# Reordering the first batch and cutting the last output tile in two halves instead of three pieces: linear attention followed by a gated feed-forward, one core

## The chip, the cores and the metric

The kernel runs on one core of a Trainium2 chip. The metric is device time in microseconds. Before the change the median of three runs is 296.06 us (295.66 to 296.08). Where the text gives a moment, it is in us from the start of the profiled span.

## What is computed

Eight batches of eight heads, 576 positions, 64 features a head. Cosine and sine weights of the position turn relu(q) and relu(k) into features of twice the width; attention is linear, so only a small matrix kv per head is needed. The result, one row of 512 per token, goes through a feed-forward with a gate.

```python
def phi(x, c, s):
    r = np.maximum(x, 0.0)
    return np.concatenate([r * c, r * s], axis=-1)
q_p = phi(q, cos_w, sin_w)
k_p = phi(k, cos_w, sin_w)
kv = np.einsum('bhsf,bhsd->bhfd', k_p, v)
z = np.sum(k_p, axis=2)
num = np.einsum('bhsf,bhfd->bhsd', q_p, kv)
den = np.einsum('bhsf,bhf->bhs', q_p, z)[..., None] + 1e-06
attn = num / den                       # then (tokens 4608, 512) as x
h = x @ w_in                           # 512 x 2048
g = h * (1.0 / (1.0 + np.exp(-beta * h)))
out = g @ w_out                        # 2048 x 512
```

## The kernel before

**Tiles and stages.** The 4608 tokens go through the feed-forward in nine chunks of 512. A chunk takes 32 slots: slots 0 to 15 make h for one of the 16 blocks of 128 columns of w_in (`h_mm`, four matmuls of 128x512 each, then a Silu on ScalarE, `h_act`), slots 16 to 31 multiply with w_out (`o_part`, four matmuls each; four parts for each of four token tiles, with the copy of the result by ScalarE and two stores after the fourth). Attention of the next batch is laid between those slots. In chunk 0 the parts come first: slots 16 to 19 use w_out slice 0 for all four tiles, 20 to 23 slice 1, 24 to 27 slice 2, 28 to 31 slice 3.

**Order.** The program's order is written out by hand; each engine works through its own instructions in that order and waits on semaphores. All loads and the last chunks' stores go through SP's queue, the other stores through GpSimd's.

**The first batch.** Nothing can be laid beside it, so its attention is written out in lines 420 to 491. The heads come in pairs: a pair jp has the heads 2jp and 2jp+1 of one half of the partitions, and the other half of the partitions (g) holds the other heads. A position is (partition, n) with n from 0 to 8. The pieces, for pairs 0 and 1:

- `v_scale` writes cos times v and sin times v (tile vb); `k_relu` writes relu(k) (tile rk); both are split over VectorE, ScalarE and GpSimd.
- `kv_mm` (line 254) multiplies them into kv: for every n two heads jj and two halves g, four matmuls of 64x64 with 130 columns, on the four quarters of the array. `kv_take` copies the result out of PSUM.
- `num_mm` multiplies the turned q with kv, `x_rden` (VectorE) forms the reciprocal of the denominator, `x_mul` (VectorE) or `x_mul_act` (ScalarE) the quotient xs, and `x_turn_pe` turns it on TensorE, with copies by ScalarE to xt, the input of h_mm.
- `warm_pe` issues matmuls of zeros in between whose result nobody reads.

**The weights of w_in.** Four slices of 512 columns (win0 to win3) come as f32 into a stage of four buffers (w_stage) and are cast to bf16 by `cast_win`. A slice is cast in pieces: gj = (g, jj) are the four pieces that hold all partitions, f0 to f1 the columns, jps the pairs of row blocks. The first two matmuls of an h_mm (mi = 0, 2) read the pieces with g = 0, mi = 1 and 3 those with g = 1. Slice 0 is cast by GpSimd, except for its last quarter; slices 1 to 3 by VectorE in halves of the columns (`cast_halves`, line 493): the first half of a slice serves two blocks jt, the second half the next two. The four slices of w_out use the same stage, slice i after w_in slice i has been cast out of its buffer; line 93 loads them, and `cast_wout` scales them to bf16.

**The last tile.** `o_last` (line 400) takes the last token tile of the last chunk in pieces of 256, 128 and 128 columns, each with 16 matmuls, a copy and two stores of 64 rows. Its stores go out on SP and on ScalarE's queue (`two=True`).

Of the kernel before, what the change touches and what calls it, by code (L numbers as in the profile page):

```python
# [17 lines left out]
NQ = 9  # L18
# [4 lines left out]
def kernel(  # L23
# [14 lines left out]
    nc = tc.nc  # L38
# [26 lines left out]
    ps = psum.tile([P, 8, 512], FP32, name="ps")  # L65
# [4 lines left out]
    def raw_tile(b, name):  # L70
        if (name, b) not in raws:
            raws[name, b] = raw_pool.tile([P, 4, NQ, D], FP32, name=f"raw_{name}", tag=f"raw_{name}")
        return raws[name, b]
# [24 lines left out]
    def cast_win(i, gj, eng="dve", f0=0, f1=512, jps=slice(0, 2)):  # L98

        g, jj = gj  # L100
        o = win[i].rearrange("q (jp g) f -> q jp g f", g=2)[jj * HP : (jj + 1) * HP, jps, g, f0:f1]
        a = stages["in", i].rearrange("q (jp jj) f -> q jp jj f", jj=2)[g * HP : (g + 1) * HP, jps, jj, f0:f1]
        if eng == "act":
            nc.scalar.copy(o, a)
        elif eng == "pool":
            nc.gpsimd.tensor_copy(o, a)
        else:
            nc.vector.tensor_copy(o, a)  # L108
# [11 lines left out]
    GJ = [(0, 0), (0, 1), (1, 0), (1, 1)]  # L120
# [65 lines left out]
    def relu(dst, src, eng):  # L186
        if eng == "act":
            nc.scalar.activation(dst, src, AF.Relu)  # L188
        else:
            nc.vector.tensor_scalar(dst, src, scalar1=0.0, scalar2=None, op0=ALU.max)  # L190

    def q_relu(b, jp, eng="dve"):
        relu(qb[:, jp].rearrange("q n (j d) -> q j n d", j=2), raw_tile(b, "q")[:, 2 * jp : 2 * jp + 2], eng)

    def k_relu(b, j0=0, j1=4, eng="dve", n0=0, n1=NQ):
        relu(rk.rearrange("q n j d -> q j n d")[:, j0:j1, n0:n1], raw_tile(b, "k")[:, j0:j1, n0:n1], eng)

    def v_scale(b, cs, jp=None, n0=0, n1=NQ, eng="dve"):
        t = (cos9, sin9)[cs]
        rv = raw_tile(b, "v")  # L200
        js = slice(0, 4) if jp is None else slice(2 * jp, 2 * jp + 2)
        if jp is not None and eng != "act":
            if eng == "dve":
                t = ps[:, 0, 16 * cs : 16 * cs + NQ]
            (nc.gpsimd if eng == "pool" else nc.vector).tensor_tensor(
                vb[:, n0:n1, js, cs, 0:D],
                rv.rearrange("q j n d -> q n j d")[:, n0:n1, js],
                t[:, n0:n1].unsqueeze(2).unsqueeze(3).to_broadcast([P, n1 - n0, 2, D]), op=ALU.mult)
            return
        for n in range(n0, n1):  # L210
            o, a = vb[:, n, js, cs, 0:D], rv[:, js, n, :]
            if eng == "act":
                nc.scalar.activation(o, a, AF.Copy, scale=t[:, n : n + 1])  # L213
            else:
                nc.vector.tensor_scalar(o, a, scalar1=t[:, n : n + 1], scalar2=None, op0=ALU.mult)  # L215
# [35 lines left out]
    def kv_out(jp, bank):  # L251
        return ps[:, bank : bank + 2, jp * 2 * E : (jp + 1) * 2 * E]

    def kv_mm(b, jp, bank, jjs=(0, 1)):
        t = kv_out(jp, bank)
        for n in range(NQ):
            for jj in jjs:
                for g in range(2):
                    hs = slice(g * HP, (g + 1) * HP)
                    nc.tensor.matmul(  # L260
                        t[jj * HP : (jj + 1) * HP, g], lhsT=rk[hs, n, 2 * jp + jj, :],
                        rhs=vb[hs, n, 2 * jp + jj].rearrange("q s e -> q (s e)"),
                        start=(n == 0), stop=(n == NQ - 1))

    def kv_take(jps, bank, eng="dve"):
        a0, a1 = jps[0], jps[-1] + 1
        o = kv[:, :, a0:a1].rearrange("q g s c e -> q g (s c e)")
        a = ps[:, bank : bank + 2, a0 * 2 * E : a1 * 2 * E]
        if eng == "act":
            nc.scalar.copy(o, a)  # L270
        else:
            nc.vector.tensor_copy(o, a)  # L272

    def num_mm(n, jp, bank, slot):

        for cs in range(2):
            for jj in range(2):
                rows = slice(jj * HP, (jj + 1) * HP)
                for g in range(2):
                    cols = slice(g * HP, (g + 1) * HP)  # L280
                    nc.tensor.matmul(  # L281
                        ps[cols, bank + jj, slot * E : (slot + 1) * E],
                        lhsT=(qt, qs)[cs][rows, jp, n, cols],
                        rhs=kv[rows, g, jp, cs, :],
                        start=(cs == 0), stop=(cs == 1))

    def x_rden(bank, slot, n0, n1, jps):

        w, m = len(jps), n1 - n0
        nv = ps[:, bank : bank + 2, slot * E : (slot + w * m) * E].rearrange("q j (i s e) -> q j i s e", s=w, e=E)  # L290
        den = small.tile([P, 2, m, w], FP32, name="den", tag=f"den{m}{w}")
        nc.vector.tensor_tensor(  # L292
            den, nv[:, :, :, :, D],
            eps9[:, n0:n1].unsqueeze(1).unsqueeze(3).to_broadcast([P, 2, m, w]), op=ALU.add)
        rden = small.tile([P, 2, m, w], FP32, name="rden", tag=f"rden{m}{w}")
        nc.vector.reciprocal(rden, den)
        return nv, rden, n0, jps
# [11 lines left out]
    def x_mul_act(got, n):  # L309
        nv, rden, first, jps = got  # L310
        for s_, jp in enumerate(jps):
            for jj in range(2):
                nc.scalar.activation(xs[:, n, jp, jj * D : (jj + 1) * D], nv[:, jj, n - first, s_, 0:D],
                                     AF.Copy, scale=rden[:, jj, n - first, s_ : s_ + 1])
# [64 lines left out]

    out_v = out.rearrange("(b p n) m -> b n p m", b=B, n=NQ)  # L380

    def store(c, tt, o_sb, m0=0, m1=512, two=False):
        for hf in range(2):
            bb, n = divmod((c * TCH + tt * P) // HP + hf, NQ)
            eng = (nc.sync, nc.scalar)[hf] if two else nc.sync if c >= 7 else nc.gpsimd
            eng.dma_start(out=out_v[bb, n][:, m0:m1], in_=o_sb[hf * HP : (hf + 1) * HP, m0:m1])  # L386

    def o_part(c, tt, part):
# [11 lines left out]
    def o_last(c, tt):  # L400

        o_sb = osb_pool.tile([P, DM], FP32, name="o_sb", tag="o_sb")
        for i, (m0, m1) in enumerate(((0, 256), (256, 384), (384, 512))):
            o_ps = ps[:, 4 + i, 0 : m1 - m0]
            for jt in range(JT):
                nc.tensor.matmul(o_ps, lhsT=gs[c, jt][:, tt * P : (tt + 1) * P],  # L406
                                 rhs=wout[jt // 4][:, jt % 4, m0:m1],
                                 start=(jt == 0), stop=(jt == JT - 1))
            (nc.scalar.copy if i == 1 else nc.vector.tensor_copy)(o_sb[:, m0:m1], o_ps)  # L409
            store(c, tt, o_sb, m0, m1, two=True)  # L410


    def warm_pe(count, w=512, bank=1):
        for i in range(count):
            nc.tensor.matmul(ps[:, bank, 0:w], lhsT=zeros[:, 0:P], rhs=zeros[:, 0:w], start=True, stop=True)  # L415
# [24 lines left out]
    warm_pe(7)  # L440
    take("act", 0)
    take("dve", 1)
    v_scale(0, 1, 0, 0, 6, eng="pool")
    take("act", 1)
    v_scale(0, 1, 0, 6, NQ, eng="act")
    v_scale(0, 0, 0)
    k_relu(0, 0, 2, "act", 0, 5)
    k_relu(0, 0, 2, "dve", 5, NQ)
# [4 lines left out]
    kv_take((0,), 6, eng="act")  # L453
    v_scale(0, 1, 1, 5, NQ, eng="act")
    k_relu(0, 2, 3, "act")
    k_relu(0, 3, 4, "act", 5, NQ)
    for i in range(1, 4):
        load_w("in", i)
    warm_pe(1)
    for n in range(7):  # L460
        num_mm(n, 0, 2, n)
    num_mm(7, 0, 4, 0)
    got = x_rden(2, 0, 0, 7, (0,))
    got2 = x_rden(4, 0, 7, 8, (0,))
    k_relu(0, 3, 4, "dve", 0, 5)
    warm_pe(2, bank=1)
    kv_mm(0, 1, 6)
    kv_take((1,), 6, eng="act")
    x_mul(got, 0, 7)
    x_mul_act(got2, 7)  # L470
    warm_pe(1, bank=1)
    for n in range(7):
        num_mm(n, 1, 0, n)
    num_mm(7, 1, 6, 0)
    for gj in GJ:
        cast_win(0, gj, "pool", jps=slice(0, 1))
    for gj in GJ:
        cast_win(0, gj, "pool", 0, 256, slice(1, 2))
    x_turn_pe(0, 0, 8, 2, jps=(0,))
# [1 line left out]
    x_mul(got, 0, 4)  # L481
    x_mul(got, 4, 7)
    x_mul(x_rden(6, 0, 7, 8, (1,)), 7, 8)
    warm_pe(3, bank=3)
    x_turn_pe(0, 0, 4, 4, ("act",), (1,))
    h_mm(0, 0, (0, 1))
    x_turn_pe(0, 4, 8, 5, ("act",), (1,))
# [5 lines left out]
    def cast_halves(i):  # L493
        for f in (0, 256):
            for gj in GJ:
                cast_win(i, gj, "dve", f, f + 256)
# [3 lines left out]
    def rest():  # L500

        x_mul(x_rden(2, 0, 8, NQ, (0, 1)), 8, NQ)
        cast_halves(2)
        cast_halves(3)
        load_w("out", 0)
        load_w("out", 1)
        load_raw(1, "v")
        load_raw(1, "k")
        load_w("out", 2)
        load_raw(1, "q")  # L510
        load_w("out", 3)
        cast_wout(0)
        cast_wout(1)
        v_scale(1, 0)
        k_relu(1)
        cast_wout(2)
        q_relu(1, 0)
# [111 lines left out]
```

## Time and profile before

| | us |
|---|---|
| median of three runs | 296.06 |
| profiled execution | 296.08 |
| its span | 294.27 |
| TensorE busy | 284.1 |
| idle of TensorE in the records from 18 us to the end, largest: before 56.58 | 0.49 |
| the same before 45.99 (w_out slice 3) | 0.22 |

| stretch, us | what runs | PE busy | DVE busy | ACT busy | POOL busy | DMA share |
|---|---|---|---|---|---|---|
| 7 to 12 | q turns, v and k of pair 0 | 3.69 | 4.46 | 3.65 | 1.47 | 1.03 |
| 12 to 17 | kv and num of both pairs | 3.98 | 3.83 | 3.28 | 3.22 | 1.04 |
| 17 to 33 | h of chunk 0 | 15.88 | 15.24 | 12.37 | 2.05 | 1.04 |
| 33 to 60 | output of chunk 0, batch 1 | 25.53 | 21.10 | 15.48 | 4.33 | 0.92 |
| 200 to 285 | last chunks | 84.52 | 9.08 | 40.05 | 12.64 | 0.28 |
| 285 to 295 | last tile, stores, end | 5.80 | 0.72 | 0.85 | 0.00 | 0.34 |

The loads of the first batch land one after the other: v of pair 0 at 8.80, k of pair 0 at 10.29, v of pair 1 at 12.07, k of head 2 at 12.73, of head 3 at 13.47, w_in slice 0 at 14.82 and 16.17, slices 1 to 3 at 18.87, 21.80 and 24.52; w_out slices at 27.36, 30.07, 38.78 and 45.19. A share of one in the table means that all 16 DMA engines work all the time. In the second table an engine's figure is its busy time within the stretch.

### The profile page before, as it was taken

To read this page: it belongs to the slowest core of one execution; us is meant where nothing else is said; L and a number is where in the kernel's file an instruction comes from. 1 tells how busy PE (TensorE), PEld (TensorE's weight loads), DVE (VectorE), ACT (ScalarE), POOL (GpSimd) and SP (SyncE) were. 2 spreads that over 40 slices of the span, in tenths; PEclk is the share of its full clock that TensorE was granted. 3 is DMA by queue.
4 is the path that set the end of the run, shared out by engine and by line. 5 is a ranking of instruction groups with operands and counts; after the bars stand their busy time and mean duration, and the time that the engine had idled before them with its cause. 6 is when DMAs were issued, how large, how long until landed. Compare 5 with 4: busy or idle time off the path is not lost.

```text
span 294.3 us, 7183 instructions
## 1 busy us (share of the span) xinstructions
PE 284.1 (97%) x3046; PEld 143.2 (49%) x3074; DVE 116.6 (40%) x297; ACT 140.1 (48%) x223; POOL 73.8 (25%) x88
## 2 busy tenths in 40 slices
PE   8799999999999999999999999999999999999995
PEld 7454455455444544454444544554455444444444
DVE  5989968662920294009500860077005000000000
ACT  5768826572248214831384128511761177127611
POOL 1350003252382026402460156014701210000000
PEclk9999999999999999999999999999999999999999
DMA  7999999597898089925992599239201910131033
GB/s 258 373 391 381 389 390 391 192 286 275 159 280 348 2 110 222 374 86 111 210 392 79 102 226 379 82 63 181 64 2 33 159 37 0 38 71 36 0 73 72
DMA packets 50416, 53.82 MB, mean 183 GB/s; under 512 B 30912, under 2 KB 31312, under 8 KB 50384
## 3 DMA queue, kind: packets, MB, share of 16 engines
q1 hardware_dynamic: 47424, 45.88, 51.7%
q0 software_dynamic: 2688, 7.34, 10.1%
q8 instruction: 24, 0.39, 0.5%
q10 hardware_dynamic: 272, 0.14, 0.2%
q14 instruction: 8, 0.07, 0.1%
HBM read 36.71 MB, written 9.44 MB: 157 GB/s over the span
## 4 chain that ended last, share of the span: by engine, by line
PE 84%; DVE 5%; DMA 5%; ACT 2%; issue 2%
PE ps L366 38%; PE ps L391 37%; DMA w_stage<-in_moe_w_out_dram 5%; DVE win L108 4%; PE ps L281 4%; PE ps L260 3%; PE ps L406 1%; PE ps L415 1%; ACT vb L213 1%; DVE qs L218 1%; DVE xs L303 0%; ACT g_t L373 0%; ACT rk L188 0%; PE ps L424 0%; PE ps L230 0%
## 5 line engine op out<-in xcount | busy, mean ns | idle before, releaser
L366 PE MATMUL ps<-xt,win 128*128 128x512 bf16 x576 | 128.1, 379 | 0.7 <-ACT g_t L373 0.5
L391 PE MATMUL ps<-wout,g_t 128*128 128x512 bf16 x535 | 120.4, 379 | 2.5 <-issue 1.4
L373 ACT ACTIVATE g_t<-ps,beta 128x512 bf16<-128x512 f32 x144 | 98.5, 688 | 36.5 <-PE ps L366 36.5
L366 PEld LDWEIGHTS <-win 128*128 128x128 bf16 x576 | 55.3, 98 | 67.5 <-DVE win L108 1.4
L391 PEld LDWEIGHTS <-g_t 128*128 128x128 bf16 x560 | 54.0, 98 | 64.0 <-issue 0.5
L386 POOL DMA_DIRECT2D out_dram<-o_sb x56 | 36.5, 656 | 142.2 <-ACT o_sb L397 142.2
L397 ACT COPY o_sb<-ps 128x512 f32<-128x512 f32 x35 | 20.5, 587 | 98.2 <-PE ps L391 98.2
L218 POOL TENSOR_TENSOR qs<-qt,tanr 128x1152 bf16<-128x1152 bf16 x12 | 29.2, 2456 | 10.3 <-DVE vb L215 8.9
L272 DVE CAST kv<-ps 128x520 bf16<-128x520 f32 x6 | 4.2, 699 | 67.8 <-PE ps L260 67.8
L409 DVE COPY o_sb<-ps 128x256 f32<-128x256 f32 (+1 forms) x2 | 0.7, 358 | 62.6 <-PE ps L406 62.6
L303 DVE TENSOR_TENSOR xs<-ps,rden 128x768 bf16<-128x768 f32 (+5 forms) x26 | 23.1, 890 | 0.8
L292 DVE TENSOR_TENSOR den<-ps,eps 128x12 f32<-128x12 f32 (+4 forms) x26 | 4.2, 161 | 33.5 <-PE ps L281 33.5
L215 DVE TENSOR_SCALAR vb<-raw_v,cos 128x256 bf16<-128x256 f32 x63 | 17.1, 348 | 0.0
L215 DVE TENSOR_SCALAR vb<-raw_v,sin 128x256 bf16<-128x256 f32 x54 | 14.7, 350 | 0.0
L281 PEld LDWEIGHTS <-qt 64*64 64x64 bf16 x576 | 10.6, 106 | 5.0 <-issue 4.3
L281 PE MATMUL ps<-kv,qt 64*64 64x65 bf16 x576 | 11.8, 194 | 0.4 <-ACT kv L270 0.2
L190 DVE TENSOR_SCALAR qb<-raw_q 128x1152 bf16<-128x1152 f32 x16 | 11.4, 753 | 1.3 <-DMA raw_q<-in_q_dram 1.3
L108 DVE CAST win<-w_stage 64x512 bf16<-64x512 f32 (+1 forms) x28 | 11.6, 413 | 0.6
L281 PE MATMUL ps<-kv,qs 64*64 64x65 bf16 x576 | 11.6, 193 | 0.0
L260 PE MATMUL ps<-vb,rk 64*64 64x130 bf16 x576 | 10.0, 218 | 1.6 <-ACT rk L188 1.6
L260 PEld LDWEIGHTS <-rk 64*64 64x64 bf16 x576 | 8.5, 106 | 5.6 <-issue 3.0
L281 PEld LDWEIGHTS <-qs 64*64 64x64 bf16 x576 | 10.4, 105 | 0.0
(56 smaller groups left out, 99.3 us busy)
## 6 DMA issues: line engine op xcount, KB each, us to landing
raw_v<-in_v_dram SPq DMA_DIRECT2D x7, 1152.0 KB, 10.3
raw_k<-in_k_dram SPq DMA_DIRECT2D x7, 1152.0 KB, 12.7
raw_q<-in_q_dram SPq DMA_DIRECT2D x7, 1152.0 KB, 7.5
out_dram<-o_sb POOLq DMA_DIRECT2D x56, 128.0 KB, 4.0
w_stage<-in_moe_w_out_dram SPq DMA_DIRECT2D x4, 1024.0 KB, 9.1
w_stage<-in_moe_w_in_dram SPq DMA_DIRECT2D x3, 1024.0 KB, 13.0
out_dram<-o_sb SPq DMA_DIRECT2D x14, 128.0 KB, 2.3
raw_q<-in_q_dram SPq DMA_DIRECT2D x2, 576.0 KB, 4.4
```

The source lines that it names most:

```text
L108: nc.vector.tensor_copy(o, a)
L190: nc.vector.tensor_scalar(dst, src, scalar1=0.0, scalar2=None, op0=ALU.max)
L215: nc.vector.tensor_scalar(o, a, scalar1=t[:, n : n + 1], scalar2=None, op0=ALU.mult)
L218: eng.tensor_tensor(dst.rearrange("q n (g p) -> q n g p", g=2), src.rearrange("q n (g p) -> q n g p", g=2), tanr[:, n0:n1].unsqueeze(2).to ...
L260: nc.tensor.matmul(t[jj * HP : (jj + 1) * HP, g], lhsT=rk[hs, n, 2 * jp + jj, :], rhs=vb[hs, n, 2 * jp + jj].rearrange("q s e -> q (s e)") ...
L281: nc.tensor.matmul(ps[cols, bank + jj, slot * E : (slot + 1) * E], lhsT=(qt, qs)[cs][rows, jp, n, cols], rhs=kv[rows, g, jp, cs, :], start ...
L303: nc.vector.tensor_tensor(o.rearrange("q j n s d -> q j (n s) d"), nv[:, :, a:z, :, 0:D].rearrange("q j n s d -> q j (n s) d"), rden[:, :, ...
L366: nc.tensor.matmul(ps[:, h_bank(c, jt)], lhsT=win[jt // 4][:, mi, (jt % 4) * P : (jt % 4 + 1) * P], rhs=xt[:, :, jp, g * HP : (g + 1) * HP ...
L373: nc.scalar.activation(g_t, ps[:, h_bank(c, jt)], AF.Silu, scale=beta[:, jt : jt + 1])
L386: eng.dma_start(out=out_v[bb, n][:, m0:m1], in_=o_sb[hf * HP : (hf + 1) * HP, m0:m1])
L391: nc.tensor.matmul(o_ps, lhsT=gs[c, jt][:, tt * P : (tt + 1) * P], rhs=wout[jt // 4][:, jt % 4, :], start=(jt == 0), stop=(jt == JT - 1))
L397: nc.scalar.copy(o_sb, o_ps)
```

## The change

Six edits. (1) `v_scale` of the sine of pair 0 is one GpSimd instruction over all n; before, GpSimd did n = 0 to 5 and ScalarE n = 6 to 8 in three. (2) `kv_mm` of pair 1 is called once for each head; the call for head 2 comes before the ScalarE part of `k_relu` for head 3 in the program, and before `x_rden`. (3) `x_mul_act` comes ahead of `kv_take` of pair 1. (4) One of the GpSimd casts of w_in slice 0 goes to ScalarE. (5) Two warm matmuls are left out. (6) The last slice of w_in is cast in four whole pieces instead of eight halves. The last output tile is computed in two pieces of 256 columns, the first copied by ScalarE and the second by VectorE, and all its stores go through SP.

```diff
-    def store(c, tt, o_sb, m0=0, m1=512, two=False):
+    def store(c, tt, o_sb, m0=0, m1=512):
         for hf in range(2):
             bb, n = divmod((c * TCH + tt * P) // HP + hf, NQ)
-            eng = (nc.sync, nc.scalar)[hf] if two else nc.sync if c >= 7 else nc.gpsimd
+            eng = nc.sync if c >= 7 else nc.gpsimd
             eng.dma_start(out=out_v[bb, n][:, m0:m1], in_=o_sb[hf * HP : (hf + 1) * HP, m0:m1])
...
-        for i, (m0, m1) in enumerate(((0, 256), (256, 384), (384, 512))):
-            o_ps = ps[:, 4 + i, 0 : m1 - m0]
+        for hf in range(2):
+            m0, m1 = 256 * hf, 256 * hf + 256
+            o_ps = ps[:, 4 + hf, 0:256]
             for jt in range(JT):
...
-            (nc.scalar.copy if i == 1 else nc.vector.tensor_copy)(o_sb[:, m0:m1], o_ps)
-            store(c, tt, o_sb, m0, m1, two=True)
+            (nc.scalar.copy if hf == 0 else nc.vector.tensor_copy)(o_sb[:, m0:m1], o_ps)
+            store(c, tt, o_sb, m0, m1)
...
-    v_scale(0, 1, 0, 0, 6, eng="pool")
+    v_scale(0, 1, 0, eng="pool")
     take("act", 1)
-    v_scale(0, 1, 0, 6, NQ, eng="act")
...
     k_relu(0, 2, 3, "act")
-    k_relu(0, 3, 4, "act", 5, NQ)
...
     num_mm(7, 0, 4, 0)
+    warm_pe(2, bank=1)
+    kv_mm(0, 1, 6, (0,))
+    k_relu(0, 3, 4, "act", 5, NQ)
     got = x_rden(2, 0, 0, 7, (0,))
     got2 = x_rden(4, 0, 7, 8, (0,))
     k_relu(0, 3, 4, "dve", 0, 5)
-    warm_pe(2, bank=1)
-    kv_mm(0, 1, 6)
+    kv_mm(0, 1, 6, (1,))
+    x_mul_act(got2, 7)
     kv_take((1,), 6, eng="act")
     x_mul(got, 0, 7)
-    x_mul_act(got2, 7)
-    warm_pe(1, bank=1)
...
     for gj in GJ:
-        cast_win(0, gj, "pool", jps=slice(0, 1))
+        cast_win(0, gj, "act" if gj == (1, 1) else "pool", jps=slice(0, 1))
...
-    warm_pe(3, bank=3)
+    warm_pe(2, bank=3)
...
         cast_halves(2)
-        cast_halves(3)
+        for gj in GJ:
+            cast_win(3, gj)
```

## The prediction

> **What bounds the kernel now.** I read the page first (busy shares, then the chain), then the first 50 us engine by engine in the timeline, the waits of the stretches that the change touches, and the last 8 us.
>
> ```profile
> PE 284.1 (97%) x3046; PEld 143.2 (49%) x3074; DVE 116.6 (40%) x297; ACT 140.1 (48%) x223; POOL 73.8 (25%) x88
> PE 84%; DVE 5%; DMA 5%; ACT 2%; issue 2%
> ```
>
> TensorE is busy 97% of the span and carries 84% of the chain. From about 18 us on it has hardly a gap, so the change can act in three places only: before 18 us, at the few waits of the first batch, and behind the last matmul. The waits of the first batch, by three views (waits of 25 to 34 us; chain of waits; timeline of PE):
>
> ```profile
> PEld L366 <- DVE win L108: 1.4, 4, 0.4
> ```
> ```profile
> 30.99 0.42 DVE win L108
> 31.41 0.03 issue
> 31.44 13.76 DMA w_stage<-in_moe_w_out_dram
> 45.20 0.02 issue
> 45.22 0.73 ACT wout L115
> ```
> ```profile
> 25.79 7.37 PE L366 MATMUL ps<-xt,win 128*128 128x512 bf16 x32
> 32.99 6.21 PE L391 MATMUL ps<-wout,g_t 128*128 128x512 bf16 x27
> ...
> 45.99 1.02 PE L391 MATMUL ps<-wout,g_t 128*128 128x512 bf16 x4 [0.22 <-ACT wout L115]
> ```
>
> Two things are to be seen. The weight loads of h_mm wait for VectorE's casts of w_in: in the single instructions jt 8 stands from 25.78 to 26.15, and each later pair of jt starts just as its half slice is ready (first half of slice 3 cast at 29.64, second matmul of jt 12 at 29.69). So VectorE and TensorE run neck and neck there. And at slot 28 PE stands 0.22 us for the last w_out slice. DMA is at 9 tenths in every slice from 26 to 50 us, moving 390 GB/s: that landing (45.2) is set by the bytes ahead of it.
>
> The casts that matter, timeline of DVE, then the two groups at 18.3 to 20 us:
>
> ```profile
> 18.50 5.07 DVE L108 CAST win<-w_stage 64x256 bf16<-64x256 f32 x12
> ...
> 24.36 7.05 DVE L108 CAST win<-w_stage 64x512 bf16<-64x512 f32 x16
> 31.45 1.67 DVE L117 TENSOR_SCALAR wout<-w_stage,rbeta 128x512 bf16<-128x512 f32 x4
> ```
> ```profile
> L108 DVE CAST win<-w_stage x4: 290/362/457, 18.5 to 19.7; 64x256 bf16<-64x256 f32 x4
> ```
> ```profile
> L106 POOL CAST win<-w_stage x3: 395/397/399, 18.0 to 18.9; 64x256 bf16<-64x256 f32 x3
> ```
>
> The four VectorE casts are alike, yet the first two take 457 and 431 ns and the others 290: the first two end 0.145 us behind a GpSimd cast each.
>
> **What the skill says.** SBUF — State Buffer, "SBUF: two separate sides": GpSimd and a VectorE operation in a 2-port mode exclude each other, whoever starts first keeps the pair for the whole instruction. The trace agrees with the casts just shown. VectorE: DVE Perf Modes, the perf-mode tier table: an fp32 copy inside SBUF runs at 2 elements a cycle; here 64x256 takes 290 ns and 64x512 421, which is 0.51 ns an element on 0.16 us fixed. TensorEngine Tiling, "Key Properties": tiles work independently; here the four 64x64 matmuls of one n start 3 ns apart and the next n 57 ns later. DMA: Bandwidth & Descriptors, "Issuing engines are not separate DMA queues": a second issuing engine saves only issue time; in the last pair of stores SP and ACT issue at 291.15 and 291.16, while SP alone starts its second store 0.51 us behind the first (288.47 after 287.96).
>
> **The change, part by part.**
>
> *sin of pair 0 all on GpSimd.* Its instruction grows from 768 to 1152 elements; the two shapes in the trace (1472 and 1257 ns) give 1.68 ns an element, so 2.12 us, 8.94 to 11.06 (2.2 at the mean rate). ScalarE loses three pieces (9.75 to 10.74), so its k_relu starts with the landing of k at 10.29 instead of 10.64 and ends at 11.04 instead of 11.37. But VectorE's own k_relu (512 elements, 10.41 to 10.83 now) falls under the longer GpSimd instruction; by the lock it ends about 0.27 behind it, at 11.33. kv_mm of pair 0 starts at 11.12, stands at n=5 until 11.39, and ends at about 11.8 instead of 12.12. Bounds: 0.33 early if it goes so, 0 if the whole k_relu comes after. I take 0.25.
>
> *kv of pair 1 by single heads.* Now: head 2 is ready on ScalarE at 14.30, the matmuls start at 14.35, head 3 joins at 14.49 behind VectorE's piece (14.43), the last one starts at 14.97. After: head 2 starts at 14.10. A head alone uses two of the four tiles, so nine n take 9 x 57 ns = 0.51 us as before, and the two heads come one after the other: 14.10 + 0.54 = 14.64, + 0.46 = 15.10, 0.13 later than now (0.05 at the best, 0.4 if the 0.25 is not there). x_mul_act, two instructions, moves ahead of kv_take and fits in the 0.62 us that ScalarE stands idle there. num_mm, x_rden and x_mul of pair 1 follow in a chain, so h_mm and VectorE's casts start 0.13 later.
>
> *One piece on ScalarE, 4th cast of slice 0.* 0.6 us behind kv_take (ends 15.7), done before the turn's copy at 17.0: free. GpSimd's remaining seven casts end at 18.59 instead of 19.26, and so VectorE's first two casts take 290 instead of 457 and 431: 0.31 us gained on VectorE; nothing if the GpSimd casts don't move up. Together the casts stand 0.17 earlier.
>
> *The warm matmuls* taken out (one before num_mm, one of three before the turn) lie in waits for ScalarE (kv, 15.61) and VectorE (xs, 17.53): nothing, as PEclk stays at 9 through the 1.1 us gap before 11.42.
>
> *Last slice in whole pieces.* Eight casts of 421 ns become four of 64x1024: 0.16 + 1024 x 0.51 = 0.68 us, with 0.02 between. They begin at 27.89 - 0.17 and all four are done after 2.81, at 30.53, 0.88 before now. But jt 12 needs the first half of all four pieces: its second matmul starts at 30.58 instead of 29.69. Behind it come 15 starts of 0.216 us: o_part begins at 33.82 instead of 32.99, PE 0.83 late. PE has no other gap until slot 28, where the wait of 0.22 goes first: 0.61 us remain. The w_out load of slice 3 is issued 0.9 earlier on SP, and the loads behind it too, but the engines are full, so it lands as now. All after slot 28 hangs on PE and moves with it.
>
> *The last tile.* 32 matmuls of 256 columns end at 290.76 (16 take 1.75) instead of 290.80. VectorE copies 256 columns, 425 instead of 292 ns, until 291.22; SP starts the first store at 291.25, the second at 291.76. A second store of 2 KB rows lands 2.37 us behind its start; rows of 1 KB land 0.29 faster (1.95 against 2.24 for first stores): 291.76 + 2.08 = 293.84, against 293.23 for ScalarE's last store now: + 0.61 (0.45 to 0.75). The stores of the first half go out before.
>
> Sum: 0.61 + 0.61 = 1.2 us on the profiled execution, 294.27 span and 1.81 around it, 296.08; that is the median of the runs too (296.06). Forecast 297.3.
>
> **Rivals.**
> *Full stall:* the k_relu of pair 0 comes wholly behind GpSimd, the heads serialise at + 0.38, and the casts gain only 0.15 from the lock: PE 1.2 late at o_part, 1.0 after the wait, plus 0.65: 297.7. For it: the lock. Against it: n=0 to 4 don't need the late piece.
> *Only the tail:* something on the way to slot 28 takes up the stall, or VectorE comes out 0.6 us further ahead: + 0.0 to 0.1 and 0.6, 296.7. Against it: no PE gap but 0.22 before slot 28.
> *Not slower:* the load of w_out slice 3 lands with its issue, as the chain draws it (13.76 us behind the cast), so 0.88 earlier, and single heads bring h_mm forward as well. Slot 28 could then start at 45.1. It decides only if PE is there, 0.67 before now, so h_mm must start at 17.3 instead of 18.0 and the jt 12 stall must vanish; less the tail this is 296.0. Against it: full DMA, and head 3's piece at 14.43, which lets the last kv matmul start 0.03 earlier at the most.
>
> **How the numbers follow.** Forecast 0.62, full stall 0.18, only the tail 0.14, not slower 0.06. The forecast's own ends are 296.8 and 297.7; 296.6 to 298.0 takes in most of the two slower rivals and leaves out about 1 in 10. About 0.2% (0.6 us) can be told from no change: "only the tail" lies on that line and gives half its chance to it, "not slower" a little: slower 0.86, same 0.09, faster 0.05.
>
> **What would show it.** A PE gap of about 1 us after the first matmul of jt 12, waiting for L108; the 0.22 wait for w_out gone and its landing still at 45.2; the first VectorE casts at 290 ns; the last kv matmul near 15.1; the two last stores 0.5 apart on SP. I am wrong if a 64x1024 cast takes well under 0.68, if the kv matmuls of a single head run closer than 57 ns per n, or if the landing moves with the issue.

## The result and the profile after

| | before | after |
|---|---|---|
| median of six runs, us | 295.69 | 297.09 |
| range of the runs | 295.62 to 296.08 | 296.80 to 297.21 |
| profiled execution | 296.08 | 297.13 |
| its span | 294.27 | 295.37 |

The ratio is 1.0042 (95% interval 1.0029 to 1.0055), so the change costs 1.24 us (0.86 to 1.63). Differences in us below are ratios worked out on the 295.7 to 296.1 us of the kernel before in the same series; those read from traces belong to one profiled execution each. One of all executions, the profiled one of everything but the tail (497.35 us at 0.56 of the clock), ran slow; it is left out, and its trace is not read.

The page of the kernel after, busy shares and the chain by engine:

```profile
PE 283.1 (96%) x3028; PEld 142.8 (48%) x3056; DVE 115.9 (39%) x292; ACT 140.0 (47%) x221; POOL 74.1 (25%) x87
...
PE 87%; DVE 4%; DMA 2%; issue 2%; ACT 2%; POOL 1%; SPq 0%; DVEq 0%; POOLq 0%
```

TensorE's busy time is all but the same, and it still carries most of the chain. DMA has lost 3 points of the chain: the step through the w_out landing, 13.76 us long, is gone. What stands there now, in the chain of waits from 29 to 46 us (start, length, what):

```profile
29.14 0.69 DVE win L108
29.84 0.70 DVE win L108
30.54 0.05 issue
30.59 3.41 PE ps L366 x15
```

The chain passes through the last two of the four whole pieces of w_in slice 3, 0.69 and 0.70 us each, and from there through TensorE alone. The timeline of PE over the same stretch (start, length, engine, line, operation, count; in brackets the idle time ahead and what ended it):

```profile
25.94 3.83 PE L366 MATMUL ps<-xt,win 128*128 128x512 bf16 x17
30.59 3.41 PE L366 MATMUL ps<-xt,win 128*128 128x512 bf16 x15 [0.82 <-DVE win L108]
33.84 6.21 PE L391 MATMUL ps<-wout,g_t 128*128 128x512 bf16 x27
...
45.59 1.94 PE L391 MATMUL ps<-wout,g_t 128*128 128x512 bf16 x8
```

Seventeen matmuls, the last of them the first one of jt 12, then 0.82 us of nothing, then the other fifteen. (The four matmuls of an `h_mm` run in the order mi = 0, 1, 2, 3, so the second is the first to read the pieces with g = 1; mi = 0 and 2 are not the first two, as the part on the kernel before has it.) Two things have changed against the kernel before: that gap is new, and the 0.22 that stood ahead of slot 28 is gone, for TensorE comes to slot 28 at 46.48 and the slice is ready. In starts of the same matmul, after is 0.84 late at the first `o_part` (33.835 against 32.991), 0.48 late at slot 28 (46.476 against 45.993), 0.51 late from 54 us and 0.40 late from 83 us on. The last tile adds 0.70, which makes the 1.10 by which the spans differ. How far single executions scatter is seen in the trace of the tail alone (below), whose first batch is that of before: it runs 0.34 ahead of the kernel before at 83 us.

The first 15 us. In the kernel before, the timelines of POOL and of DVE have

```profile
8.94 1.47 POOL L205 TENSOR_TENSOR vb<-raw_v,sin 128x768 bf16<-128x768 f32 x1 [6.78 <-DMA raw_v<-in_v_dram]
```
```profile
10.41 0.42 DVE L190 TENSOR_SCALAR rk<-raw_k 128x512 bf16<-128x512 f32 x1
```

and in the kernel after:

```profile
9.22 2.11 POOL L205 TENSOR_TENSOR vb<-raw_v,sin 128x1152 bf16<-128x1152 f32 x1 [7.06 <-DMA raw_v<-in_v_dram]
```
```profile
10.56 1.06 DVE L190 TENSOR_SCALAR rk<-raw_k 128x512 bf16<-128x512 f32 x1
...
12.27 1.34 DVE L205 TENSOR_TENSOR vb<-raw_v,ps 128x1152 bf16<-128x1152 f32 x1
...
14.11 0.47 DVE L190 TENSOR_SCALAR rk<-raw_k 128x320 bf16<-128x320 f32 x1
...
18.66 4.75 DVE L108 CAST win<-w_stage 64x256 bf16<-64x256 f32 x12
24.18 6.34 DVE L108 CAST win<-w_stage 64x512 bf16<-64x512 f32 x12
30.56 2.87 DVE L117 TENSOR_SCALAR wout<-w_stage,rbeta 128x512 bf16<-128x512 f32 x7
```

GpSimd's one instruction for the sine of pair 0 waits for v of pair 0, which landed at 9.08 here and at 8.80 before, and runs until 11.33. VectorE's `k_relu` of 512 elements took 0.42 us before; it takes 1.06 now and ends at 11.62, 0.28 behind GpSimd. Everything behind it on VectorE moves: the `v_scale` of pair 1 from 12.10 to 12.27, the piece of head 3 ready at 14.58 instead of 14.43. In the other direction, the first two of the casts at 18.66 take 274 and 286 ns instead of 457 and 431, and the casts end at 30.53 instead of 31.41.

The end. SP's own timeline from 287 us on, before and after, and the DMA issues of 288 to 297 us in the kernel after (count, KB each, median us from issue to landing):

```profile
287.96 3.67 SPq L386 DMA_DIRECT2D out_dram<-o_sb  x5
```
```profile
288.36 4.45 SPq L386 DMA_DIRECT2D out_dram<-o_sb  x6
```
```profile
out_dram<-o_sb SPq DMA_DIRECT2D x4, 64.0 KB, 2.0
```

All stores of the last two tiles now stand on SP. (The stretches hold pauses: SP is not issuing all the time in them.) Counted from the first matmul of the last tile, the last two are issued at +4.20 and +4.72 and land at +6.13 and +6.76; before, they were issued at +4.05 (SP) and +4.06 (ScalarE), landed by +6.13, and the kernel ended at +7.17. It ends at +7.87 now.

### The profile page after: what moved, and what is told of

Same layout as the page of the kernel before. It is cut to its first block, busy times and chain, and to the rows that moved or that the text cites. A ratio compares the mean times of both kernels' runs of the same rounds, so it can differ in the third digit from the quotient of the medians.

```text
span 295.4 us, 7134 instructions
## 1 busy us (share of the span) xinstructions
PE 283.1 (96%) x3028; PEld 142.8 (48%) x3056; DVE 115.9 (39%) x292; ACT 140.0 (47%) x221; POOL 74.1 (25%) x87
## 4 chain that ended last, share of the span: by engine, by line
PE 87%; DVE 4%; DMA 2%; issue 2%; ACT 2%; POOL 1%; SPq 0%; DVEq 0%; POOLq 0%
PE ps L391 40%; PE ps L366 39%; DVE win L108 4%; PE ps L281 4%; PE ps L260 3%; DMA raw_v<-in_v_dram 2%; PE ps L407 1%; POOL vb L205 1%; DVE xs L303 0%; ACT vb L213 0%; ACT g_t L373 0%; PE ps L230 0%; ACT xt L345 0%; SPq L78 0%; DVE rden L296 0%
## 5 line engine op out<-in xcount | busy, mean ns | idle before, releaser
L190 DVE TENSOR_SCALAR rk<-raw_k 128x2304 bf16<-128x2304 f32 (+2 forms) x9 | 11.0, 1223 | 0.1
L108 DVE CAST win<-w_stage 64x512 bf16<-64x512 f32 (+2 forms) x24 | 10.6, 443 | 0.5
```

## The experiments

My theory is that of the prediction: the loss is the wait of jt 12 for whole pieces (less what the wait at slot 28 gives back) and the tail, and the other edits of the first batch nearly cancel. The rivals are that the first batch loses by the lock and the single heads, and that the landing of w_out slice 3 decides. Edits are against the kernel before, unless said otherwise.

**The change in its parts.** First the tail alone, that is, `store` and `o_last` of after:

```diff
-        for i, (m0, m1) in enumerate(((0, 256), (256, 384), (384, 512))):
+        for hf in range(2):
+            m0, m1 = 256 * hf, 256 * hf + 256
...
-            (nc.scalar.copy if i == 1 else nc.vector.tensor_copy)(o_sb[:, m0:m1], o_ps)
-            store(c, tt, o_sb, m0, m1, two=True)
+            (nc.scalar.copy if hf == 0 else nc.vector.tensor_copy)(o_sb[:, m0:m1], o_ps)
+            store(c, tt, o_sb, m0, m1)
```

> The kernel before, with the last tile in two halves and all its stores on SP; the first batch untouched. Theory of the prediction (tail and cast wait cost about the same): the two last stores start 0.5 us apart on SP, the last one lands 0.6 later relative to the start of the last tile, time + 0.6 us (0.45 to 0.75). Rival 'only the first batch costs': + 0.0 to 0.2. Rival 'only the tail costs': + 1.2, the whole of the change.

Measured 1.0021 (1.0012 to 1.0031), + 0.62 us. In the trace its last stores stand as in after, and the end comes at +7.86.

Then everything but the tail, which keeps its three pieces (part of the edit):

```diff
+    kv_mm(0, 1, 6, (0,))
...
-        cast_win(0, gj, "pool", jps=slice(0, 1))
+        cast_win(0, gj, "act" if gj == (1, 1) else "pool", jps=slice(0, 1))
...
-        cast_halves(3)
+        for gj in GJ:
+            cast_win(3, gj)
```

> The five edits of the first batch and the whole pieces of the last w_in slice, with the last tile in three pieces as before. Theory of the prediction: TensorE stands at jt 12 until about 30.6, slot 28 starts 0.5 to 0.6 later than in the kernel before, time + 0.4 to 0.6 us. Rival 'only the tail costs': + 0.0. Rival 'late start of h': the 0.15 us by which h starts later is carried to the end and the cast wait adds nothing to it: + 0.15.

Measured 1.0024 (1.0015 to 1.0034), + 0.71 us (0.44 to 1.0). The two parts sum to 1.33, inside the interval of the whole: nothing shows that they act on each other.

Then the first batch was parted: the whole pieces alone,

```diff
-        cast_halves(3)
+        for gj in GJ:
+            cast_win(3, gj)
```

> The kernel before, with the last w_in slice cast in four whole pieces and nothing else. Theory of the prediction: casts end at 30.7 (27.89 + 2.81), second matmul of jt 12 at 30.75, o_part starts at 34.0 instead of 32.99, of that 0.39 goes into the wait for the last w_out slice: time + 0.6 us. Rival 'the first batch's other edits cost': + 0.0 to 0.1 here, and all of the cost in the run without whole pieces.

and the first batch without them:

```diff
-        for gj in GJ:
-            cast_win(3, gj)
+        cast_halves(3)
```
(This edit is against the kernel with everything but the tail.)

> The five edits of the first batch without the whole pieces, last tile in three pieces. Theory of the prediction: h starts 0.15 later, VectorE's casts run 0.16 earlier than before, so TensorE meets no cast wait at jt 8 to 14 and comes to slot 28 as early as before or a little earlier; there it waits for the last w_out slice as before: time 0.0, between - 0.2 and + 0.1. Rival 'late start of h': + 0.15 or more. Rival 'the landing moves with the issue': - 0.3 or better, as the load is issued 0.16 earlier and TensorE is there.

Whole pieces alone: 1.0034 (1.0022 to 1.0046), + 1.0 us (0.65 to 1.36), more than the 0.6 that was expected. The rest of the first batch: 1.0002 (0.9994 to 1.0009), nothing. The timeline of PE with whole pieces alone:

```profile
31.03 3.41 PE L366 MATMUL ps<-xt,win 128*128 128x512 bf16 x15 [0.94 <-DVE win L108]
34.28 6.21 PE L391 MATMUL ps<-wout,g_t 128*128 128x512 bf16 x28
```

The gap is 0.94 here and 0.82 in after, where VectorE's first casts are free of the lock (274, 286 and 290 ns for the first three; 275, 395 and 408 here). The way from the start of h to TensorE's arrival at slot 28 takes 28.53 us here, 28.28 in after and 27.59 before. So the other edits seem to give back something of the whole pieces' cost (0.24 in these traces; between the medians 0.3, with intervals that overlap, so that it isn't settled), and nothing without them.

**Does the wait for the late pieces make up the whole cost?** The last four blocks get their mi = 0 and 2 first, which read only the two pieces that are ready early; mi = 1 and 3 follow. The last tile is that of before:

```diff
-        elif slot < 16:
+        elif slot < 12:
             h_group(0, slot)
+        elif slot < 16:
+            if slot == 12:
+                for jt in range(12, 16):
+                    h_mm(0, jt, (0, 2))
+            h_mm(0, slot, (1, 3))
+            h_act(0, slot)
```

First with the whole pieces alone, then with all edits of the first batch:

> The last w_in slice in four whole pieces, and in chunk 0 the eight matmuls of jt 12 to 15 that read the first two pieces (mi 0 and 2) ahead of the eight that read the last two (mi 1 and 3); else the kernel before. Theory of the prediction: the cost of whole pieces is the wait of jt 12 for the last two pieces; with eight matmuls (1.73 us) laid into it no wait is left, o_part starts at the time of before or up to 0.15 earlier: time 0.0 (- 0.2 to + 0.15). Rival 'longer casts cost by themselves, in VectorE or in what follows them': + 1.0, as with whole pieces alone.

> The same order of jt 12 to 15 with all edits of the first batch, last tile in three pieces: the changed kernel with both of its costs taken away. Theory of the prediction: 0.0 to - 0.3 us against the kernel before, bounded by the landing of the last w_out slice (44.5 to 45.2) and by h starting no earlier. Rival 'the edits of the first batch gain once the wait is gone': - 0.5 or better.

Measured 0.9996 (0.9987 to 1.0005) and 0.9996 (0.9986 to 1.0005). The timeline of PE in the first of the two:

```profile
25.77 7.17 PE L366 MATMUL ps<-xt,win 128*128 128x512 bf16 x32
32.77 6.21 PE L391 MATMUL ps<-wout,g_t 128*128 128x512 bf16 x27
...
46.12 1.02 PE L391 MATMUL ps<-wout,g_t 128*128 128x512 bf16 x4 [0.57 <-ACT wout L115]
```

The 32 matmuls run without a gap and the first `o_part` starts at 32.77, 0.22 earlier than before; but TensorE gives this away at slot 28, where it waits for the slice of w_out. So the + 1.0 was the wait of jt 12, and the size of a piece costs nothing measurable in itself. The new order wasn't run with the halves; in the kernel before, the matmuls of jt 12 to 15 wait 0.07 us in all, read by their starts, so the order could have brought little more than that by itself. The second version is about 0.8 us below everything but the tail, which it differs from in the order alone, and doesn't beat the kernel before measurably. Its timelines of PE and DVE show what is late next:

```profile
42.76 0.68 PE L230 MATMUL ps<-ident,qb 128*128 128x128 bf16 x9 [0.16 <-DVE qb L190]
```
```profile
41.95 1.43 DVE L190 TENSOR_SCALAR qb<-raw_q 128x1152 bf16<-128x1152 f32 x2 [1.33 <-DMA raw_q<-in_q_dram]
```

VectorE stands 1.33 us for q of batch 1 (landed at 41.92), and TensorE, which turns q, then waits for VectorE's relu of it.

**Is it the DMA?** Of w_out slice 2 a quarter is loaded, and its four casts all read that quarter; the other three quarters of that slice are left out of the computation. So w_out slice 3, q of batch 1 and all loads behind them have 0.79 MB less ahead of them:

```diff
-            nc.sync.dma_start(out=st, in_=w_out_v[:, 4 * i : 4 * i + 4, :])
+            w = 1 if i == 2 else 4
+            nc.sync.dma_start(out=st[:, 0:w], in_=w_out_v[:, 4 * i : 4 * i + w, :])
...
-            j = 4 * i + jj
+            j, js = 4 * i + jj, 0 if i == 2 else jj
```

With the kernel before, and with all edits of the first batch and the order of the last experiment:

> The kernel before, but only a quarter of w_out slice 2 is loaded (256 KB instead of 1024) and used for all four of its row blocks; work and waits of the engines stay. Everything queued behind it lands about 2 us earlier. Theory that the loads bound the first 46 us: the wait at slot 28 is gone, the rest stays, since the cast waits and the start of h are what they were: - 0.1 to - 0.3 us. Rival 'the loads don't bound': 0.0.

> The edits of the first batch with whole pieces and jt 12 to 15 reordered, last tile in three pieces, and the same quarter of w_out slice 2 alone loaded. Theory that the loads hide what these edits gain: without the wait for q of batch 1 (0.49 before the turn of slot 25) and for w_out slice 3, - 0.5 to - 0.8 us against the kernel before, clearly below the light kernel before. Rival 'the edits gain nothing anyway, as h starts when the loads of the first 13 us allow': the same as the light kernel before, within 0.15.

Measured 0.9992 (0.9985 to 0.9998), - 0.24 us, and 0.9983 (0.9975 to 0.9991), - 0.50. With the light load slot 28 doesn't wait for the slice's landing (42.78 and 42.91) in either trace: ScalarE casts the slice only when it is through with its copies of the turned q, at 44.84 and 44.89, and TensorE stands 0.02 for that. So the late loads cost the kernel before about a quarter of a us on the average of its runs. That this is the wait for w_out slice 3 is likely but not shown, since q of batch 1 and the loads of batch 2 come earlier too. What the new first batch, with the new order of jt 12 to 15, is worth when DMA is out of the way is 0.27, but the two intervals overlap, and it isn't settled.

**The tail in its parts.** Halves with the stores on two queues (that is, the tail of after with `two=True`), and three pieces as before with all stores on SP:

```diff
-            store(c, tt, o_sb, m0, m1)
+            store(c, tt, o_sb, m0, m1, two=True)
```

> The kernel before with the last tile in two halves, but the stores still on SP and ScalarE's queue. It parts the tail's cost. Theory of the prediction: of + 0.6 the second issue on SP is 0.4 and the longer copy and rows 0.2, so + 0.2 us here, the last store landing 2.2 behind its issue on ScalarE's queue. Rival 'the size of the last piece is what costs': + 0.6, as with all stores on SP.

```diff
-            store(c, tt, o_sb, m0, m1, two=True)
+            store(c, tt, o_sb, m0, m1)
```

> The kernel before with the last tile in three pieces, all its stores on SP. Theory of the prediction: a pair of stores holds SP for 1.05 us, the last two pieces are 0.6 apart, so the last pair starts behind the pair of the second piece and its second store is issued at about 291.9 instead of 291.15: + 0.6 us. Rival 'the size of the last piece is what costs': + 0.0 to 0.1, as the size is that of before.

Measured 1.0014 (1.0008 to 1.0021), + 0.41, and 1.0033 (1.0023 to 1.0044), + 0.98: both cost more than expected (0.2 and 0.6). SP's timeline with three pieces on SP alone, and the DMA issues of the halves on two queues:

```profile
287.62 5.26 SPq L386 DMA_DIRECT2D out_dram<-o_sb  x8
```
```profile
out_dram<-o_sb SPq DMA_DIRECT2D x2, 64.0 KB, 1.9
out_dram<-o_sb ACTq DMA_DIRECT2D x2, 64.0 KB, 2.2
```

From the first of the eight stores to the last SP is taken up for 5.26 us, of which it issues for 4.38. The four of the last two pieces are issued at +3.65, +4.25, +4.93 and +5.53 from the tile's first matmul, where in the kernel before the last two went at +4.05 and +4.06, and the kernel ends at +8.38: on one queue, small pieces queue behind each other, and the finer cut makes it worse. This is why halves on SP end earlier in the trace than thirds on SP (+7.86 against +8.38; by the medians + 0.62 and + 0.98, with intervals that overlap), while thirds are best on two queues. Halves on two queues issue both last stores at +4.20, land at +6.14 (SP) and +6.41 (ScalarE) and end at +7.57. Going from there to SP alone costs 0.21 by the medians, 0.30 by the ends in the traces; the larger last piece is the other 0.41, 0.40 in the traces. The expectation had these shares the other way round. The medians alone don't part them, since their intervals overlap; the traces do, for in the nine with the tail of before the kernel ends at +7.15 to +7.18. The Trainium skill (DMA: Bandwidth & Descriptors, "Issuing engines are not separate DMA queues") puts what a second issuing engine saves at the time of the issue alone, and this agrees: SP's second store is issued 0.52 behind its first, against a landing of some 2 us, and the second queue saves 0.30 of that.

**Two single edits of the first batch, read in one profiled execution each.** Only the heads of pair 1 one by one (with `k_relu` for head 3 and `x_mul_act` moved as in after), and only the cast on ScalarE:

```diff
-    kv_mm(0, 1, 6)
+    kv_mm(0, 1, 6, (0,))
+    k_relu(0, 3, 4, "act", 5, NQ)
...
+    kv_mm(0, 1, 6, (1,))
+    x_mul_act(got2, 7)
```

> Pair 1's kv by single heads and x_mul_act ahead of kv_take, else the kernel before. Theory of the prediction: from the first to the last start of the 36 matmuls 1.0 us (two times 9 x 57 ns) instead of 0.62, the last start 0.35 to 0.4 later than with both heads; the earlier start for head 2 doesn't exist here. Rival 'two tiles run closer than 57 ns per n': under 0.8 us.

```diff
-        cast_win(0, gj, "pool", jps=slice(0, 1))
+        cast_win(0, gj, "act" if gj == (1, 1) else "pool", jps=slice(0, 1))
```

> One of the four first casts of w_in slice 0 on ScalarE instead of GpSimd, else the kernel before. Theory of the prediction (GpSimd and VectorE exclude each other): GpSimd's casts end 0.65 earlier relative to VectorE's, and VectorE's first two 64x256 casts take about 290 ns each instead of 457 and 431. Rival 'the first casts are slow for another reason, their load or the start of a row of casts': above 400 ns still.

With single heads the 36 matmuls of pair 1 start from 14.35 to 15.15: 0.80 from first to last, where the two heads one after the other would have taken 1.0, and before it was 0.62. (The stretch by itself tells little: with both heads together it lies between 0.62 and 0.95 in the traces, as head 3's k comes early or late.) In the single instructions, head 2 alone moves on by 57 ns per n, as predicted; but head 3's first matmul starts 0.32 behind head 2's first, as soon as its k is there, where head 2's last starts 0.48 behind. It doesn't wait for head 2 to be through.

With the one cast on ScalarE, VectorE's first three casts take 307, 287 and 289 ns (timeline of DVE, 18 to 19.2 us):

```profile
18.57 0.61 DVE L108 CAST win<-w_stage 64x256 bf16<-64x256 f32 x2
```

This is the lock that the Trainium skill describes (SBUF — State Buffer, "SBUF: two separate sides"), taken away by itself: before, the same two casts took 888 ns. What it is worth differs between executions, since it depends on when the casts of the two engines meet: the first three took 276, 398 and 289 ns with the tail alone, and 275, 395 and 408 with whole pieces alone.

## Why the prediction was right, and where its steps were not

**The sine of pair 0.** The instruction took 2.11 us (predicted 2.12), and `k_relu` on VectorE was held until 0.28 behind it (predicted 0.27): the lock was read rightly from two casts. The step's yield was wrong: 0.25 for `kv_mm` of pair 0, found 0.03 (11.39 against 11.42), since v landed 0.28 later in that execution and the long instruction starts with that landing. Even the full gain would have bought nothing in that execution. In the kernel with the first batch but no whole pieces, v landed early and `kv_mm` of pair 0 started at 10.76, 0.66 ahead of before. Its timeline of ACT shows where that goes:

```profile
12.43 1.28 ACT L213 ACTIVATE vb<-raw_v,sin 128x128 bf16<-128x128 f32 x4 [0.54 <-DMA raw_v<-in_v_dram]
```

ScalarE stands 0.54 for v of pair 1. The prediction had h hang on `kv_mm` of pair 0 alone; the traces show two paths, and the later one decides. With the first batch of before, h starts 6.59 to 6.60 us after `kv_mm` of pair 0 in four traces (the kernel before, the tail alone, thirds on SP, whole pieces in the new order), and 5.92 to 5.93 us after v of pair 1 lands in four others (whole pieces alone, halves on two queues, the light load, the cast on ScalarE). In the profiled kernel before, the first path ended at 18.02, and the second would have at 18.00: a gain at `kv_mm` could pass on 0.02 and no more. In the three traces with the new first batch and an early v of pair 0, where `kv_mm` of pair 0 starts at 10.73 to 10.93, h hangs on v of pair 1 throughout (5.92 to 5.93). This path was missing in the prediction. In after h starts 6.14 behind that landing, by the late `k_relu`.

**Single heads.** h was to start 0.13 later, and in after it starts 0.15 later. The size is right by luck, for the reason isn't: the heads interleave, and the last piece comes late from VectorE (14.58 against 14.43), whose work was pushed back by the `k_relu` that the lock held. The last matmul of pair 1 starts 0.53 to 0.54 behind that piece in the traces with both heads together, and 0.53 to 0.56 behind it with single heads: the split itself costs 0.02 at most. The gain that failed at `kv_mm` and the cost that failed here took each other away.

**The cast on ScalarE.** The first two casts at 274 and 286 ns instead of 290, and the end of all casts at 30.53, as predicted.

**The warm matmuls.** Nothing is seen of them, though they weren't tried alone: the first batch without whole pieces costs nothing in all.

**Whole pieces.** 685 to 690 ns for one (predicted 0.68); second matmul of jt 12 at 30.59 (30.58); first `o_part` 0.84 late (0.83). Behind it the term for slot 28 was mis-sized. The prediction took the 0.22 of the profile for the wait. The profile counts idle time from the modelled end of a matmul, 379 ns after its start, while the starts in a full row are 216 ns apart; TensorE was ready at 45.61, and the wait was 0.385, of which 0.36 could be given back: 0.02 to 0.03 is left in every trace in which slot 28 doesn't wait for the load. It also took the landing as fixed at 45.2. The landing was 44.69 in after, and 44.37 to 46.04 over the traces with the full load, with no clear relation to when the load is issued: it was 45.32 with whole pieces in the new order, where it is issued as early as in after (30.61 and 30.56), and 44.37 with thirds on SP, where it is issued at 31.55. In before, 15 of the load's 16 shares had landed by 44.47, and the last came 0.73 later; what holds that share back isn't shown. So the wait that takes up part of the stall is anything from nothing to 0.73 us in an execution (the 0.57 of the profile, read by the starts). In the profiled pair it left 0.48 at slot 28, against the predicted 0.61, and 0.40 from 83 us on; 0.11 came back at 72 us, and why is open. Over all runs it left 0.71 with the rest of the first batch. That the 0.61 lies between these is in part luck, with the wait mis-sized and the landing moving by more than a us.

**The tail.** + 0.61 predicted, + 0.62 measured by the medians, 0.70 in the profiled pair. Second store 0.52 behind the first (0.51), landing 2.04 behind its issue (2.08), last landing 0.63 later than before.

Sum: 1.2 predicted, 1.24 measured, 1.10 in the profiled pair. The mechanism, a wait of jt 12 for whole pieces and at the end a larger last piece with both stores on SP, is right; that the sum is so close owes something to the terms above that cancel. Of the rivals, the full stall needed the k of pair 0 to come wholly late and the heads in a row; neither is so. Only the tail would have needed TensorE to be held up elsewhere before slot 28; with whole pieces alone the full 0.94 gap goes through (0.96 in starts at the end of that trace). That the landing would move with its issue is not seen in the landings above.

## What to carry to other kernels

Cut a cast by what its reader needs first, not by its length: the same bytes in fewer instructions took less time on VectorE and yet cost a us, because TensorE's second matmul of jt 12 had to wait for the last two of four whole pieces, where the first half of each had been enough; putting the matmuls in the order in which the pieces come took the whole cost away. Before counting a gain upstream, look for the load whose landing the next stage waits for, in more than one execution. At the end of this kernel two things counted: how large the last piece is, and how many stores stand in one queue behind the last copy; a finer cut paid only with a second queue.

## What the hardware showed that I had not expected

- A VectorE instruction held by GpSimd doesn't begin anew when it is let go: the `k_relu` of 512 elements, 0.42 us alone, ended 0.28 behind GpSimd, and the 64x256 casts of before, 0.29 alone, ended 0.145 behind. Of each, 0.14 to 0.15 us was over by then, nearly the fixed 0.16 of the prediction's price for a cast; what was left is close to 0.51 ns for each of its elements.
- Two groups of 64x64 matmuls on different quarters of the array, issued one group after the other, don't run in a row: the second group's first matmul starts 0.16 ahead of the first group's last, and each group keeps its own 57 ns per n. The Trainium skill says that tiles operate independently (TensorEngine Tiling, "Key Properties"); I hadn't carried that over to instructions that stand one behind the other in the program.
- A store of 64 rows from ScalarE's queue landed 0.27 later than the store of the tile's other 64 rows that SP issued at the same moment (+6.41 against +6.14). In part this may lie with the rows: with both on SP the second half took 2.04 from issue to landing, the first 1.93.
- The sixteen shares of one 1 MB load don't land together: in the kernel before they land from 42.72 to 45.20, the last 0.73 behind the one ahead of it, and the last share's moment differs between executions by more than a us.
